# The q of one batch moves from VectorE to TensorE, later q transfers are halved, and an order is chosen anew

## The chip, the core and the metric

The kernel runs on one core of a Trainium2 chip. The metric is device time in microseconds (us), as the median of repeated executions. A profile is one execution taken by the hardware profiler; its span goes from the first to the last instruction. The engines are TensorE (PE, with PEld for its weight loads), VectorE (DVE), ScalarE (ACT), GpSimd (POOL) and SyncE (SP), which here issues nearly all DMAs.

## What is computed

An attention block without softmax feeds a two-layer network with a softplus between.

```python
batch, n_heads, seq, head_dim = (8, 8, 576, 64)
kv = np.einsum('bhsd,bhse->bhde', k, v)
out = np.einsum('bhsd,bhde->bhse', q, kv)
rms = np.sqrt(np.mean(out * out, axis=-1, keepdims=True) + 1e-06)
attn = out / rms * g_norm
x = attn.transpose(0, 2, 1, 3).reshape(4608, 512)
h = x @ w_in                                           # 512 x 2048
g = np.maximum(h, 0.0) + np.log1p(np.exp(-np.abs(h)))
result = g @ w_out                                     # 2048 x 512
```

The inputs q, k, v and g_norm are float32, the two weights float64.

## The kernel before

**Tiles.** The 4608 rows of x are 36 tiles of 128 rows; three tiles make a block of 384 (`NT`), and there are 12 blocks. A batch has 576 rows, four tiles and a half: batch 2 is tiles 9 to 12 and half of tile 13, batch 3 the other half of tile 13 and tiles 14 to 17. `parts(t)` says which batches a tile holds. `d_ff` is cut into 16 chunks of 128.

**Steps.** The network is walked in three phases over the blocks; `ENDS` says which chunks each phase does for each block. The first four blocks do chunks 0 to 3 in phase 0. One `step` is one block with one chunk: `mm1` (twelve matmuls, L660), softplus and a split into three parts on ACT and DVE, and `mm2` (nine matmuls, L667). Both products are made of three matmuls in a reduced form of float32, so x, the weights and g are each split into three terms. Partial results go to DRAM between phases. Steps 0 to 3 belong to block 0, 4 to 7 to block 1, 12 to 15 to block 3.

**Weights.** `weight(j, ...)` fetches one chunk of w_in (even j) or w_out (odd j), here named Wj, into one of two `raw` buffers (L283), turns float64 into float32 by several operations on DVE and ACT (L294 to L324), and `divide` splits it (L356 to L378; the first eight use two TensorE matmuls, L374 and L375).

**Attention.** `kv_of(b)` loads k and v of a batch into the ring `m` (L491, and tails L489) and multiplies them on TensorE (L502). `rows(t)` makes a tile of x: it needs q with the head dimension on the partitions (`qT`), multiplies it with kv (`out_rows`, L521, 32 matmuls into one of two `o` banks), squares on ACT (L590), reduces on DVE (L525), takes the root on POOL (L528, L529) and normalizes on DVE (L533). For tiles under `BY_PE` = 12 TensorE turns x (`turn_x`, L539); ACT copies it (L599) and SP stores it for later phases (L600). Tiles of the first two blocks (`AT_ONCE` = 6) are split from the turned tile directly; the others are loaded again (L638) and split (L445, L448, L452).

**How q is turned.** In batches 0 and 1 a tile's q is loaded by itself, in two transfers of rows of 64 floats (`load`, L567), turned by four TensorE transposes (`turn_q`, L577) into bank `tp`, or `o` from tile 6 on, and copied to `qT` by ACT (L584). From batch 2 on `load_q(b)` loads a whole batch into the one buffer `qa`, in four transfers of rows of 32 floats (L423), so that DVE can turn it with blocks of 32 x 32 (L552). Those loads follow each other, and none starts before `mm1` of a step set by `behind`.

**What sets the order.** The kernel is scheduled by hand: each piece of work is a `Task` with an engine, an estimated duration, a position `pos`, the buffers it takes and gives, and the tasks it comes after. `Plan.order` goes through the tasks as a list scheduler: an engine takes a task that could start within 150 ns (`SOON`) of the earliest possible, and of these the one with the lowest position. The result is a fixed order of instructions on each engine. SP may not run further than 2.5 us ahead of an estimated end of the DMAs (`dma_free`), and each DMA has an estimated length (`size`). Where TensorE would have nothing to do ahead of step 6, the plan puts in a filler matmul (`warm`, L778) whose result nobody reads.

**Positions.** They are counted in steps; negative ones are before step 0. They come from `P0`: eight for the conversion of the first eight weights (`CONVERT`), eight for their fetches (`FETCH`), eleven offsets for the attention and the loads (`EARLY`) and thirteen for the later weights (`LATER`). For instance `x_pos(t)` is `t * EARLY[0] + EARLY[1]` in block 0, and the first step of the tile's block less `EARLY[2]` (block 1) or `EARLY[3]` (later) plus the tile's index in its block; `kv_of` stands `EARLY[4]` ahead of the batch's first tile (`EARLY[5]` for batch 0) and loads `EARLY[6]` ahead of that; q is loaded `EARLY[7]` ahead of the tile, in `load_q` ahead of the batch's second tile. A load with `behind` = n waits for `mm1` of step n; a negative n is no wait.

Of the kernel before, what the change touches and what calls it, by code (L numbers as in the profile page):

```python
# [40 lines left out]
class Plan:  # L41
# [15 lines left out]
    def slot(self, ring):  # L57
        return Slot(ring)

    def add(self, engine, ns, run, after=(), pos=0.0, take=(), give=(), size=0, behind=None, follows=None):  # L60
        t = Task(engine, ns, run, [a for a in after if a is not None], pos, list(take), list(give), size)
        for s in t.give:
            s.readers += 1
        self.tasks.append(t)
        t.follows = follows
        t.behind = behind
        return t
# [79 lines left out]
def kernel(  # L147
# [25 lines left out]
    B, H, S, D = q.shape  # L173
# [3 lines left out]
    NP = H // 2  # L177
# [9 lines left out]
    PLACES = 8  # L187
    LAST = PHASES[-1]

    P0 = [-93.0, 0.8, -33.3, -5.7, -14.1, 1.5, -43.9, 2.2, -65.0, -42.8, -62.7, -19.7, -30.7, -6.2,  # L190
          -2.2, -4.7, 2.5, -26.5, 18.0, 10.5, 5.5, 8.5, -2.0, 2.5, 3.5, 25.5, -16.5, 10.0, 6.5, 41.0,
          52.0, 65.5, 54.5, 72.0, 91.5, 94.5, 115.5, 106.0, 111.5, 8.5]
    CONVERT, FETCH, EARLY, LATER = P0[:8], P0[8:16], P0[16:27], P0[27:]
    BY_PE = 12
    AT_ONCE = 2 * TB
# [27 lines left out]
    slot, add = plan.slot, plan.add  # L223

    def new(s, shape, dtype=F32):
        if s.ring == "o":
            s.tile = o_banks[:, :, s.place]
            return s.tile
        pool = ps if s.ring in PS else sb
        s.tile = pool.tile(shape, dtype, tag=f"{s.ring}_{s.place}", name=f"{s.ring}_{s.place}")  # L230
        return s.tile

    def pairs(x, p):

        return x[:, 2 * p:2 * p + 2].rearrange("r h d -> r (h d)")


    def halves(src, e):

        return src[e * NP:(e + 1) * NP].rearrange("p s d -> s p d")  # L240
# [155 lines left out]
    def parts(t):  # L396

        b, s0 = divmod(t * P, S)
        if s0 + P <= S:
            return [(b, 0, P, s0)]  # L400
        return [(b, 0, S - s0, s0), (b + 1, S - s0, P - S + s0, 0)]
# [8 lines left out]
    BL = 32  # L410
    q_slots, q_loads = {}, {}

    def load_q(b):


        q_slots[b], q_loads[b] = slot("qa"), []
        pos = x_pos(first_tile[b] + 1) - EARLY[7]

        def run(e, c):
            if not (e or c):  # L420
                new(q_slots[b], [P, NP * S])
            r0 = BL * (2 * e + c)
            nc.sync.dma_start(  # L423
                out=q_slots[b].tile[r0:r0 + BL].rearrange("j (i d) -> j i d", d=BL),
                in_=q[b, e * NP:(e + 1) * NP, :, BL * c:BL * (c + 1)].rearrange("p (i j) d -> j (p i) d", j=BL))

        for e in range(2):
            for c in range(2):
                q_loads[b].append(add("SP", 450, lambda e=e, c=c: run(e, c), (), pos + 0.2 * (2 * e + c),
                                      [q_slots[b]] if not (e or c) else [], [], 2190, behind=int(pos) - 3,  # L430
                                      follows=q_loads[b][-1] if e or c else None))

    def split(ph, t, x, ready, pos):
        n, i = divmod(t, TB)
# [33 lines left out]
    def x_pos(t):  # L468

        n = t // TB  # L470
        return t * EARLY[0] + EARLY[1] if n == 0 else first_step[0, n] - (EARLY[2] if n == 1 else EARLY[3]) + t % TB
# [36 lines left out]
    def rows(t):  # L508
        pos = x_pos(t)
# [31 lines left out]
        def part_of_qT(n, r0):  # L541
            if qT.tile is None:
                new(qT, [P, NP, P])
            return qT.tile[:, :, r0:r0 + n]

        turned = []
        for b, r0, n, s0 in parts(t):
            if b >= 2:
                if b not in q_slots:
                    load_q(b)  # L550
                turned.append(add(
                    "DVE", 690 if n == P else 420, lambda b=b, r0=r0, n=n, s0=s0: nc.vector.transpose(  # L552
                        out=part_of_qT(n, r0),
                        in_=q_slots[b].tile.rearrange("k (p s) -> k p s", p=NP)[:, :, s0:s0 + n]),
                    q_loads[b], pos - 1, [qT] if not r0 else [], [q_slots[b]], follows=turned[-1] if turned else None))
                continue

            if 0 not in q_slots:
                q_slots[0] = slot("qa")
            at_qa = n == P and b == 0  # L560
            q_s = q_slots[0] if at_qa else slot("m")

            def load(b=b, n=n, s0=s0, q_s=q_s, at_qa=at_qa):
                if q_s.tile is None:
                    new(q_s, [P, NP * S] if at_qa else [P, H, D])
                for e in range(2):
                    nc.sync.dma_start(out=natural(q_s, at_qa)[:n, e::2], in_=halves(q[b, :, s0:s0 + n], e))  # L567

            def natural(q_s, at_qa):
                if not at_qa:  # L570
                    return q_s.tile
                return q_s.tile[:, t * d_model:(t + 1) * d_model].rearrange("s (h d) -> s h d", d=D)

            def turn_q(n=n, q_s=q_s, at_qa=at_qa, tp=slot("tp" if t < AT_ONCE else "o")):
                y = new(tp, [P, NP, P])
                for p in range(NP):
                    nc.tensor.transpose(y[:, p, :n], pairs(natural(q_s, at_qa)[:n], p), ident[:n, :n])  # L577

            tp = turn_q.__defaults__[-1]
            ld = add("SP", 900, load, (), pos - EARLY[7], [q_s] if not at_qa or t == 0 else [], [], 1220 * n // P,  # L580
                     behind=int(pos) - 3, follows=first_load[0] if t and at_qa else None)
            first_load.append(ld)
            a = add("PE", 440, turn_q, [ld], pos - 1, [tp], [q_s])
            turned.append(add("ACT", 590, lambda n=n, r0=r0, tp=tp: nc.scalar.copy(part_of_qT(n, r0), tp.tile[:, :, :n]),  # L584
                              [a], pos - 1, [qT] if not r0 else [], [tp], follows=turned[-1] if turned else None))
        need = [u for pt in parts(t) for u in kv_ready[pt[0]]]
        a = o_task = add("PE", 640, out_rows, turned + need, pos, [o], [qT])
        for pt in parts(t):
            o_tasks.setdefault(pt[0], []).append(a)
        a = add("ACT", 600, lambda: nc.scalar.activation(new(x, [P, H, D]).rearrange("s (a k) d -> s a (k d)", k=2), o.tile, func=AF.Square,  # L590
                                                              scale=D ** -0.5), [a], pos, [x])
        a = add("DVE", 690, reduce, [a], pos, [r])
        a = add("POOL", 2300, root, [a], pos)
        a = add("DVE", 700, norm, [a, o_task], pos, [], [o, r])
        if t < BY_PE:
            a = add("PE", 440, turn_x, [a], pos + 0.5, [xp], [x])
            if t < AT_ONCE:
                split(0, t, xp, a, pos + 0.5)
            a = add("ACT", 600, lambda: nc.scalar.copy(new(xg, [P, KD, P]), xp.tile), [a], pos + 1, [xg], [xp])  # L599
            x_there[t] = [add("SP", 450, lambda: nc.sync.dma_start(  # L600
                out=x_of(t), in_=xg.tile), [a], pos + 1, [], [xg], 1000)]
# [4 lines left out]
        n, i = divmod(t, TB)  # L606
        g = TB if n < n_blocks - 1 else 1
        i0, i = i - i % g, i % g
# [21 lines left out]
    def x_of(t):  # L630

        n, i = divmod(t, TB)
        return xd[n][:, i * P:(i + 1) * P].rearrange("(a p) t -> p a t", p=P)
# [120 lines left out]
    for c in range(KF):  # L754
        for j in (2 * c, 2 * c + 1):
            pos = CONVERT[j] if c < 4 else LATER[c - 4] + LATER[12] * (j % 2)
            weight(j, pos, FETCH[j] if c < 4 else pos)
    for b in range(B):
        kv_of(b)
        for t in range(n_tiles):  # L760
            if parts(t)[-1][0] == b:
                rows(t)
# [51 lines left out]
```

## Time and profile before

| | us |
|---|---|
| median of 11 runs | 908.09 |
| lowest and highest of them | 907.17, 912.96 |
| the profiled execution | 912.96 |
| its span | 911.2 |
| `mm1` matmuls, L660, 2304 of them, busy | 436.3 |
| `mm2` matmuls, L667, 1728 of them, busy | 433.5 |
| filler, L778, 53 of them, busy | 20.5 |
| start of the first `mm1` | 42.66 |
| DVE transposes of q, L552, 24 whole, 6 halves, mean ns | 690, 427 |
| ACT copies of turned q, L584, from `tp`, from `o`, mean ns | 586, 594 |
| q of a batch, L423, 24 transfers of 288 KB, median us to landing | 7.3 |
| q of a tile, L567, into `m`: 8 of 128 KB and 4 of 64 KB, median us to landing | 4.3, 7.5 |

Busy times of TensorE contain overlaps at both ends of a group, and a matmul's duration is longer than its distance from the next. The row of a group names the line, the engine, what is written and read, and how many; in the chain of waits a piece is one after which the next could begin. The profiled execution is the longest of the eleven.

### The profile page before, as it was taken

Reading aid. Unit: us, or ns where it says so; the run is one execution under the profiler, and the core shown is the slowest. Engines: PE = TensorE matmul, PEld = TensorE weight load, DVE = VectorE, ACT = ScalarE, POOL = GpSimd, SP = SyncE. Lnnn points to the kernel's source line nnn. Section 1 sums busy time; section 2 is a strip of 40 time slices with the busy share of each in tenths; the row PEclk is TensorE's granted clock in tenths of the full one; section 3 lists DMA queues with packets and bytes.
Section 4 is the critical chain, followed back from the end, with each engine's and each line's share of the span. In section 5 each row is a group of like instructions: output and inputs, shape, how many; then the busy total and the mean of one; then the engine's idle time right before and its main releaser. Section 6 shows DMA issues by size and latency. Waiting matters only on the chain.

```text
span 911.2 us, 15563 instructions
## 1 busy us (share of the span) xinstructions
PE 895.5 (98%) x5983; PEld 790.7 (87%) x5983; DVE 624.0 (68%) x1054; ACT 408.3 (45%) x788; POOL 84.3 (9%) x79
## 2 busy tenths in 40 slices
PE   7899999999999999999999999999999999999998
PEld 5678888888888888999899998989999998999996
DVE  6786988676577877888668787886534555555553
ACT  5675654534444556654435544554323333333331
POOL 0433422223113200000000000000000000000000
PEclk8999999999999999999999999999999999999999
DMA  9999989479681635355343444741330433333323
GB/s 242 258 204 264 252 182 239 96 177 190 177 175 37 168 101 185 104 172 175 104 127 128 151 143 157 230 148 39 105 103 2 139 105 104 105 104 104 104 73 102
DMA packets 211451, 131.58 MB, mean 144 GB/s; under 512 B 102320, under 2 KB 185264, under 8 KB 211376
## 3 DMA queue, kind: packets, MB, share of 16 engines
q1 hardware_dynamic: 211216, 130.58, 52.7%
q8 instruction: 47, 0.77, 0.4%
q14 instruction: 28, 0.23, 0.1%
q10 hardware_dynamic: 160, 0.00, 0.0%
HBM read 91.75 MB, written 38.80 MB: 143 GB/s over the span
## 4 chain that ended last, share of the span: by engine, by line
PE 94%; DMA 4%; DVE 1%; ACT 0%; SPq 0%; issue 0%; DVEq 0%
PE h L660 45%; PE s L667 44%; DMA m<-in_v_dram 3%; PE o_banks L521 2%; PE tp L502 2%; DMA raw<-in_moe_w_in_dram 1%; DMA g_col<-in_g_norm_dram 1%; PE h L778 0%; PE o_banks L539 0%; DMA m<-in_k_dram 0%; PE tp L539 0%; SPq L491 0%; PE s L502 0%; ACT m L599 0%; PE tp L577 0%
## 5 line engine op out<-in xcount | busy, mean ns | idle before, releaser
L660 PE MATMUL h<-xv,w 128*128 128x384 f32 x2304 | 436.3, 338 | 0.2 <-ACT w L378 0.2
L667 PE MATMUL s<-w,gv 128*128 128x512 f32 x1728 | 433.5, 395 | 0.0
L660 PEld LDWEIGHTS h<-xv,w 128*128 128x128 f32 x2304 | 407.2, 188 | 16.4 <-ACT w L378 0.4
L667 PEld LDWEIGHTS s<-w,gv 128*128 128x128 f32 x1728 | 319.7, 188 | 60.4 <-DVE gv L675 0.2
L682 ACT ACTIVATE g<-h 128x384 f32<-128x384 f32 x192 | 94.3, 491 | 403.8 <-PE h L660 402.0
L671 DVE TENSOR_TENSOR gv<-g,gv 128x384 fp32r<-128x384 f32 x192 | 106.5, 554 | 181.1 <-ACT gv L684 180.0
L684 ACT ACTIVATE gv<-g 128x384 fp32r<-128x384 f32 x192 | 100.8, 525 | 24.7 <-PE s L667 18.5
L675 DVE SCALAR_TENSOR_TENSOR gv<-gv 128x384 fp32r<-128x384 f32 x192 | 106.8, 556 | 5.8
L448 DVE SCALAR_TENSOR_TENSOR xv<-m,g_col,xv 128x512 fp32r<-128x512 f32 x102 | 76.0, 745 | 2.3 <-ACT xv L445 2.3
L452 DVE SCALAR_TENSOR_TENSOR xv<-xv 128x512 fp32r<-128x512 f32 x108 | 74.3, 688 | 2.5
L445 ACT ACTIVATE xv<-m,g_down 128x512 fp32r<-128x512 f32 x102 | 70.1, 711 | 2.4 <-DMA m<-x 2.3
L529 POOL TENSOR_TENSOR r<-r,half 128x8 f32<-128x8 f32 x36 | 66.1, 1835 | 3.0
L533 DVE TENSOR_TENSOR x<-o_banks,r 128x512 f32<-128x512 f32 x36 | 24.8, 689 | 20.7 <-POOL r L529 8.4
L709 DVE SCALAR_TENSOR_TENSOR m<-s,scale,m 128x512 f32<-128x512 f32 x24 | 17.9, 747 | 29.7 <-PE s L667 29.7
L528 POOL TENSOR_SCALAR r<-r 128x8 f32<-128x8 f32 x36 | 17.3, 480 | 220.7 <-DVE r L525 220.3
L709 DVE SCALAR_TENSOR_TENSOR m<-s,m 128x512 f32<-128x512 f32 x36 | 23.7, 685 | 7.8 <-PE s L667 7.8
L521 PEld LDWEIGHTS o_banks<-kv,m 64*64 64x64 f32 x1152 | 20.2, 135 | 9.7 <-issue 5.5
L311 ACT ACTIVATE sq<-sq,big 128x512 bf16<-128x512 bf16 x32 | 22.9, 715 | 10.7 <-DVE m L307 10.7
L525 DVE TENSOR_REDUCE r<-x 128x8 f32<-128x512 f32 x36 | 24.2, 678 | 4.7 <-ACT x L590 4.7
L359 DVE TENSOR_TENSOR m<-m,w 128x512 f32<-128x512 f32 x30 | 20.6, 686 | 9.2 <-ACT w L356 8.8
L590 ACT ACTIVATE x<-o_banks 128x512 f32<-128x512 f32 x36 | 21.1, 593 | 12.5 <-PE o_banks L521 7.2
L521 PE MATMUL o_banks<-kv,m 64*64 64x64 f32 x1152 | 24.9, 226 | 0.8 <-ACT m L584 0.7
(71 smaller groups left out, 430.7 us busy)
## 6 DMA issues: line engine op xcount, KB each, us to landing
m<-x SPq DMA_DIRECT2D x102, 256.0 KB, 4.7
part<-m SPq DMA_DIRECT2D x72, 256.0 KB, 2.6
m<-part SPq DMA_DIRECT2D x72, 256.0 KB, 3.9
raw<-in_moe_w_in_dram SPq DMA_DIRECT2D x16, 512.0 KB, 5.3
m<-in_k_dram SPq DMA_DIRECT2D x32, 256.0 KB, 4.9
m<-in_v_dram SPq DMA_DIRECT2D x32, 256.0 KB, 4.8
raw<-in_moe_w_out_dram SPq DMA_DIRECT2D x16, 512.0 KB, 5.6
qa<-in_q_dram SPq DMA_DIRECT2D x24, 288.0 KB, 7.3
```

Of the source, the lines that this page charges most:

```text
L445: nc.scalar.activation(cols(0, F32R), x.tile, func=AF.Identity, scale=g_down)
L448: nc.vector.scalar_tensor_tensor(out=cols(1, F32R), in0=x.tile, scalar=g_col, in1=cols(0), op0=ALU.mult, op1=ALU.subtract)
L452: nc.vector.scalar_tensor_tensor(out=cols(2, F32R), in0=cols(1), scalar=-RADIX, in1=cols(0), op0=ALU.mult, op1=ALU.add)
L521: nc.tensor.matmul(y[r0:r0 + P // 2, a, c0:c0 + D], lhsT=qT.tile[e * D:(e + 1) * D, p, r0:r0 + P // 2], rhs=kvs[b % 2][e * D:(e + 1) * D, ...
L529: nc.gpsimd.tensor_tensor(out=r.tile, in0=r.tile, in1=half, op=ALU.pow)
L660: nc.tensor.matmul(hp, lhsT=w_in.tile[:, i, kd * P:(kd + 1) * P], rhs=xv.tile[:, i, kd], start=(m == 0), stop=(m == 3 * KD - 1))
L667: nc.tensor.matmul(mine[i].tile, lhsT=gv.tile[:, m, i * P:(i + 1) * P], rhs=w_out.tile[:, m], start=(c == cs[0] and m == 0), stop=(c == cs ...
L671: nc.vector.tensor_tensor(out=gv.tile[:, 1], in0=g.tile, in1=gv.tile.bitcast(F32)[:, 0], op=ALU.subtract)
L675: nc.vector.scalar_tensor_tensor(out=gv.tile[:, 2], in0=f32[:, 1], scalar=-RADIX, in1=f32[:, 0], op0=ALU.mult, op1=ALU.add)
L682: a = add("ACT", 490, lambda: nc.scalar.activation(new(g, [P, NT]), h.tile, func=AF.Softplus, scale=1.0 + E), [a], s, [g], [h])
L684: a = add("ACT", 530, lambda: nc.scalar.activation(new(gv, [P, 3, NT], F32R)[:, 0], g.tile, func=AF.Copy, scale=DOWN), [a], s, [gv])
L709: a = add("DVE", 700, lambda: nc.vector.scalar_tensor_tensor(out=new(ot, [P, d_model]), in0=bank.tile, scalar=(scale if ph == LAST else 1. ...
```

## The change

Three edits. `load_q` makes eight transfers a batch instead of four: each of the four groups of 32 partitions (`a`) is filled in two transfers of two head pairs (`p`), and the plan is told half the length for each. Its batches begin with 3 instead of 2, so the q of batch 2 is loaded and turned in the way of batches 0 and 1: five parts, each with two transfers, four TensorE transposes and an ACT copy, in the ring `m` and, for the turned tile, an `o` bank. And 23 of the 40 numbers in `P0` are different.

```diff
-    P0 = [-93.0, 0.8, -33.3, -5.7, -14.1, 1.5, -43.9, 2.2, -65.0, -42.8, -62.7, -19.7, -30.7, -6.2,
-          -2.2, -4.7, 2.5, -26.5, 18.0, 10.5, 5.5, 8.5, -2.0, 2.5, 3.5, 25.5, -16.5, 10.0, 6.5, 41.0,
-          52.0, 65.5, 54.5, 72.0, 91.5, 94.5, 115.5, 106.0, 111.5, 8.5]
+    P0 = [-88.5, 0.8, -46.3, -8.2, -11.1, 2.0, -42.9, 2.7, -64.0, -43.8, -63.7, -16.7, -31.2, -9.7, 0.3,
+          -4.7, 5.0, -33.5, 16.5, 10.5, 5.5, 8.5, -2.0, 2.5, 3.5, 26.0, -22.0, 10.0, 4.5, 41.0, 50.0,
+          65.5, 54.5, 72.0, 91.5, 94.5, 114.5, 106.0, 109.5, 8.5]
...
-        def run(e, c):
-            if not (e or c):
+        def run(a, p):
+            if not (a or p):
                 new(q_slots[b], [P, NP * S])
-            r0 = BL * (2 * e + c)
+            e, c = divmod(a, 2)
             nc.sync.dma_start(
-                out=q_slots[b].tile[r0:r0 + BL].rearrange("j (i d) -> j i d", d=BL),
-                in_=q[b, e * NP:(e + 1) * NP, :, BL * c:BL * (c + 1)].rearrange("p (i j) d -> j (p i) d", j=BL))
-
-        for e in range(2):
-            for c in range(2):
-                q_loads[b].append(add("SP", 450, lambda e=e, c=c: run(e, c), (), pos + 0.2 * (2 * e + c),
-                                      [q_slots[b]] if not (e or c) else [], [], 2190, behind=int(pos) - 3,
-                                      follows=q_loads[b][-1] if e or c else None))
+                out=q_slots[b].tile[BL * a:BL * (a + 1), p * S:(p + 2) * S].rearrange("j (i d) -> j i d", d=BL),
+                in_=q[b, e * NP + p:e * NP + p + 2, :, BL * c:BL * (c + 1)].rearrange("p (i j) d -> j (p i) d", j=BL))
+
+        for a in range(4):
+            for p in range(0, NP, 2):
+                q_loads[b].append(add("SP", 500, lambda a=a, p=p: run(a, p), (), pos + 0.1 * (2 * a + p // 2),
+                                      [q_slots[b]] if not (a or p) else [], [], 1095, behind=int(pos) - 3,
+                                      follows=q_loads[b][-1] if a or p else None))
...
-            if b >= 2:
+            if b >= 3:
```

## The prediction

> **What bounds the kernel now.** I read the page's busy rows and its 40 slices first, then busy time by stretch, then the chain of waits, then the instructions of SP and of TensorE in order of time.
>
> ```profile
> PE 895.5 (98%) x5983; PEld 790.7 (87%) x5983; DVE 624.0 (68%) x1054; ACT 408.3 (45%) x788; POOL 84.3 (9%) x79
> PE   7899999999999999999999999999999999999998
> DMA  9999989479681635355343444741330433333323
> ```
>
> TensorE sets the time: 895.5 of 911.2 us. The DMA engines are full in the first slices and loose later. Where TensorE still has room is seen by stretch (columns: length; busy us of PE, PEld, DVE, ACT, POOL; granted clock; DMA share; GB/s):
>
> ```profile
> 0.00:42.00 42.00, 33.31 (x373) 22.75 (x373) 29.25 (x53) 23.07 (x44) 10.34 (x15) 0.88 0.95 247
> 42.00:76.40 34.40, 32.05 (x372) 26.49 (x373) 26.78 (x46) 23.56 (x48) 9.89 (x8) 0.95 0.97 229
> 76.40:130.00 53.60, 53.49 (x604) 45.98 (x604) 45.09 (x77) 32.39 (x62) 17.96 (x16) 1.00 0.90 233
> 130.00:260.00 130.00, 130.00 (x1216) 112.02 (x1214) 93.65 (x158) 55.35 (x107) 32.18 (x28) 1.00 0.79 174
> ```
>
> From 76.4 us on TensorE has no gap. Part of its earlier busy time is filler: `warm` (L778). The same stretches for that line alone (busy us of PE, PEld; clock; DMA):
>
> ```profile
> 0.00:42.00 42.00, 18.44 (x47) 9.70 (x47) 0.88 0.95 247
> 42.00:76.40 34.40, 2.03 (x7) 1.05 (x6) 0.95 0.97 229
> ```
>
> So the room is 8.7 idle + 18.4 filler = 27.1 us before the first `mm1` (42.7 us), and 2.35 + 2.03 = 4.4 us from there to 76.4. Nothing that only moves work after 76.4 us can shorten the run, and each TensorE instruction added there lengthens it. The chain of waits (start, length, what) shows what ended last in the second stretch:
>
> ```profile
> 59.61 0.54 SPq L491
> 60.15 0.05 issue
> 60.20 0.02 SPq L491
> 60.21 0.03 issue
> 60.24 7.38 DMA m<-in_v_dram
> 67.62 0.14 issue
> 67.75 0.69 PE tp L502 x16
> 68.44 3.37 PE h L660 x12
> 71.81 1.05 PE tp L502 x16
> ```
>
> A load of v, issued at 60.24, lands at 67.62; TensorE's kv matmuls (L502) wait for it, and `mm1` of step 3 stands behind them. SP's issues tell why v was late:
>
> ```profile
> 49.86 0.45 SPq L491 DMA_DIRECT2D m<-in_v_dram  x1
> 50.36 6.82 SPq L423 DMA_DIRECT2D qa<-in_q_dram  x2
> 57.28 1.20 SPq L600 DMA_DIRECT2D x<-m  x1
> 58.57 0.45 SPq L491 DMA_DIRECT2D m<-in_k_dram  x1
> ...
> 60.71 6.40 SPq L423 DMA_DIRECT2D qa<-in_q_dram  x2
> ```
>
> The four transfers of batch 2's q hold SP for 6.82 + 6.40 = 13.2 us; k and v of the same batch stand behind the first two.
>
> **What the change does, part by part.** Batch 2 is rows 1152 to 1727: tiles 9 to 12 whole and half of tile 13, five parts.
>
> *TensorE, added.* Five `turn_q`, 20 transposes. Four of them are 0.44 us on the chain behind other transposes and 0.62 behind other matmuls; 5 x 0.44 to 5 x 0.62 is 2.2 to 3.1 us. I take 2.6, between the two because both neighbours occur. They fall around and after 60 us; if they land in a gap that is left, they cost nothing, so the range goes from 0 to 3.1. The Trainium skill, "TensorE: Matmul & The Clock Gate", Part 4 (PE-mode transpose), gives about 275 ns for a 128x128 transpose inside a kernel; 20 x 0.275 would be an estimated 5.5 us and with it the change would come out level. This trace has one each 0.11 to 0.155 us, and the row is nearer than the page.
>
> *ACT, added; DVE, removed.* The copies at L584 take 0.585 to 0.599 us (0.37 for a half): 4 x 0.59 + 0.37 = 2.7 us on ACT, busy 6.4 of 10 us at 80 to 90. DVE loses 4 x 0.69 + 0.43 = 3.2 us of L552 between 74 and 87 us. TensorE has its next work in hand there, so I cost both at nothing; without this cover the one takes 2.7 and the other gives 3.2.
>
> *DMA, the main term.* From 50.4 to 67.2 us the windows give 193, 197 and 189 GB/s, about 3.2 MB, where 269 GB/s follow from 68 to 80. The q of a batch is 1.18 MB; the other 2.0 MB at 269 GB/s need 7.5 us, so q took some 9.3 us in rows of 128 bytes. By tiles, in rows of 256 bytes, only tiles 9 to 11 are loaded early: 0.79 MB at the 241 GB/s of 30 to 50 us, 3.3 us. Tiles 12 and 13 get places 3 and 4 and may start only after `mm1` of steps 2 and 3. So about 6 us of DMA leave the stretch 50 to 67 us, and v, now 1.7 us late, is there in time. What then goes: 1.74 idle at 66.0, about 0.2 more of idle there, 2.03 of filler, and the slow clock behind the gap (granted 0.55 in 69 to 72 us: `mm1` 3.37 for 2.28 us, L502 1.05 for 0.62, together 1.5). Sum 5.5 us at most. I take all of it, since the cover needed (1.7 us of DMA) is a third of what leaves.
>
> *Eight transfers a batch.* SP issues 10 + 40 where it issued 24: 26 more by 0.43 to 0.51 us, 11 to 13 us spread to about 260 us, while TensorE is without a gap. Cost nothing; if the cover were gone, some 0.5 us for each that stands before a load that is waited for. Batch 3's q is different: the `qa` buffer, read last by the turns at 31 us, is now free for it, its place is 5.0 and it waits only for `mm1` of step 2 (51.3 us), where before it was issued from 87.75 us. The Trainium skill ("DMA: Bandwidth & Descriptors", Bandwidth) asks for transfers of 1 MiB and calls small ones descriptor-dominated, which speaks against halving 288 KB, with no price for two that overlap. In SP's rows two of the 288 KB transfers were issued within 2.91 us at 92.45, while one takes 7.3 us (median) to land: they overlap, and I let the split cost no more than the same packets before.
>
> *Buffers.* q of tiles 9 to 13 now takes places of the 13-deep ring `m` and a third use of the two `o` banks. Behind a waiting `out_rows` or `turn_q` stand `mm1` and `mm2`, in TensorE's one queue. Tiles 6 to 8 already use the banks so; their waits are 0.2 us (0.21 at 62.72). Five times that is 1.0 us above, nothing below; I take nothing, as tile 9's rows are needed only at step 12.
>
> *Positions.* By rank, most of the start stays: W0, W2, W1, k and v of batch 0, W4 with q of tiles 0 to 2, W3, batch 1. Three things shift: the W4 conversion goes from before the rows of tile 3 (-14.1 against -14.0) to behind tile 4 (-11.1 against -11.5); W5's fetch is earlier (-6.2 to -9.7); W6's fetch, issued at 49.39, goes behind batch 2's k and v and the q of tiles 9 and 10 (-2.2 to 0.3). The trace has no run of this order. Bounds: in the instructions of DVE and TensorE tile 1 is normalized at 31.2 and turned only at 34.4, behind kv of batch 1 that waits 1.69 us for its v, and tile 2 is normalized at 38.3 and turned at 39.6: 3.1 + 1.2 = 4.3 us to gain at most; on the other side a W4 pushed by two tiles' reduce and norm (2 x 1.4 us on DVE) is 2.8 us of loss. I take nothing: `mm1` 0 needs neither W4 nor W5.
>
> **Sum.** Profiled execution 912.96 us, of which the span is 911.2 and 1.8 lies around it: 912.96 - 5.5 + 2.6 = 910.1. The median of the 11 runs is 908.09, 4.9 below the profiled one; the difference of -2.9 carried to it gives **905.2**.
>
> **Rivals.** *The relief is given back* (chance 0.20). SP takes whatever has its buffer, and batch 3's q needs no place in `m`: it may fill the hole that batch 2's q leaves, with 9.3 us of packets beside the 3.3 of the tiles. For it: `qa` is free and the wait is only on step 2. Against it: its place, 5.0, is behind all of batch 3's k and v. Then half of the 5.5 is won and 2.6 paid: 908.0.
>
> *A weight comes late; slower* (0.28). W6 now is fetched at 49.39 and its last conversion on ACT (L378) ends at 64.7, 3.7 us before `mm1` of step 3 starts. Issued behind k and v of batch 2, that is at 60.2, it would be 10.8 us later and `mm1` 3 would wait 10.8 - 3.7 = 7.1 us; other TensorE work fills about half. With the 2.6 of turns: 908.1 + 3.5 + 2.6 = 914 at worst, 911.5 if half of the 5.5 is still won. It decides from a fetch of W6 later than about 53 us. Against it: its raw buffer and SP are free while k and v wait for places in `m`.
>
> *The start gains as well* (0.17): the turn of tile 1 no longer stands behind kv of batch 1, 3.1 us more: 902.1. For it, their places are now 5 apart and earlier by 4.5 and 2; against it, their rank did not change.
>
> *My forecast* has 0.35. About 0.2%, 1.8 us, is what a measurement of this kernel can tell from no change. Faster takes the forecast, but for a small part, and the third rival: 0.50; same 0.20; slower 0.30. The likeliest case alone runs from 902.6 (5.5 won, nothing paid) to 907.5; the whole range, with the bounds of the positions, **900 to 912**.
>
> **What would show it.** Right: 20 more matmuls at L577; the L502 of batch 2 without a wait for v; no filler and a granted clock near 1.00 from 60 to 76 us; TensorE without a gap by about 73 us. Wrong: batch 3's q issued before 70 us with SP held for several us at L423; W6's fetch after 53 us and `mm1` of step 3 waiting for ACT; new TensorE waits at `o_banks`; a first `mm1` more than 3 us away from 42.7, which would make the positions the main term; or gaps after 80 us, of which I cost none.

## The result: slower by half a per cent, and the profile after

The changed kernel takes 912.71 us (median of 11 runs, 911.79 to 915.62); the kernel before, over 41 runs, 908.36. The ratio is 1.0048, 95% interval [1.0036, 1.0060]: 4.4 us slower, and above the predicted 900 to 912. The profiled executions say the opposite at first sight: a span of 910.6 after, 911.2 before. The page of the kernel after, busy rows and slices:

```profile
PE 898.0 (99%) x6005; PEld 790.9 (87%) x6005; DVE 621.9 (68%) x1049; ACT 411.5 (45%) x793; POOL 85.6 (9%) x79
PE   7999999999999999999999999999999999999998
DMA  9999767959681636355343445650320433433323
```

TensorE is busy for 2.5 us more, DVE for 2.1 less. By stretch of the kernel after (length; busy us of PE, PEld, DVE, ACT, POOL; clock; DMA share; GB/s):

```profile
0.00:42.00 42.00, 34.59 (x389) 24.45 (x390) 31.85 (x58) 25.16 (x48) 10.95 (x15) 0.92 0.99 262
42.00:76.40 34.40, 33.92 (x420) 27.72 (x422) 29.66 (x50) 25.66 (x52) 12.30 (x10) 1.00 0.99 250
76.40:130.00 53.60, 52.81 (x606) 43.87 (x597) 42.78 (x72) 33.22 (x64) 18.40 (x16) 1.00 0.80 214
130.00:260.00 130.00, 130.00 (x1193) 111.42 (x1184) 88.31 (x149) 53.19 (x102) 29.97 (x26) 1.00 0.78 170
```

and for the fillers, L778, alone (busy us of PE, PEld; clock; DMA):

```profile
42.00:76.40 34.40, 2.45 (x8) 1.42 (x8) 1.00 0.99 250
```

From 42 to 76.4 us the idle time fell as forecast, to 0.48 us, and the granted clock stays at 1.00. But there are eight fillers now, not none, and from 76.4 to 130 there is 0.79 us of idle where there was 0.11. The instructions of TensorE after (start, us, what, idle before and its releaser) show the place:

```profile
68.64 0.60 PE L539 MATMUL o_banks<-ident_r,x 128*128 128x128 f32 x4
68.99 1.83 PE L778 MATMUL h<-ident_r 128*128 128x512 f32 x6
71.03 0.66 PE L577 MATMUL o_banks<-ident_r,m 128*128 128x128 f32 x4 [0.21 <-ACT m L599]
...
77.96 0.66 PE L577 MATMUL o_banks<-ident_r,m 128*128 128x128 f32 x4 [0.31 <-ACT x L590]
```

The turned x of a tile occupies an `o` bank until ACT has copied it (L599); `turn_q` of the next tile stands in TensorE's queue for that bank. Six fillers and 0.21 us of idle precede it at 71.0. The wait at 77.96 ends with another reader of these banks, ACT's squares (L590). SP's issues after, of the q loads among others:

```profile
48.34 1.34 SPq L423 DMA_DIRECT2D qa<-in_q_dram  x1
49.77 2.45 SPq L491 DMA_DIRECT2D m<-in_k_dram  x1
52.28 0.86 SPq L423 DMA_DIRECT2D qa<-in_q_dram  x1
...
56.84 0.67 SPq L423 DMA_DIRECT2D qa<-in_q_dram  x1
57.62 0.97 SPq L283 DMA_DIRECT2D raw<-in_moe_w_in_dram  x1
...
65.32 0.47 SPq L423 DMA_DIRECT2D qa<-in_q_dram  x1
```

Half of batch 3's q, four of its eight transfers, is in the hole that batch 2's left, as one rival said, but one transfer at a time: a q load holds SP for 1.34 us at most in these rows, where two of them held it for 6.82 and 6.40 us before.

### The profile page after: what moved, and what is told of

It is laid out like the page before. It is cut to its first block, busy times and chain, and to the rows that moved or that the text cites. A ratio compares the mean times of both kernels' runs of the same rounds, so it can differ in the third digit from the quotient of the medians.

```text
span 910.6 us, 15638 instructions
## 1 busy us (share of the span) xinstructions
PE 898.0 (99%) x6005; PEld 790.9 (87%) x6005; DVE 621.9 (68%) x1049; ACT 411.5 (45%) x793; POOL 85.6 (9%) x79
## 4 chain that ended last, share of the span: by engine, by line
PE 96%; DMA 2%; ACT 1%; issue 0%; DVE 0%; SPq 0%; DVEq 0%
PE h L660 45%; PE s L667 44%; PE o_banks L521 2%; PE tp L502 2%; DMA m<-in_v_dram 2%; PE h L778 1%; PE s L502 1%; PE o_banks L577 0%; PE o_banks L539 0%; PE tp L539 0%; PE h L374 0%; PE tp L577 0%; ACT m L584 0%; ACT x L590 0%; ACT m L599 0%
## 5 line engine op out<-in xcount | busy, mean ns | idle before, releaser
L521 PEld LDWEIGHTS o_banks<-kv,m 64*64 64x64 f32 x1152 | 20.1, 134 | 8.9 <-issue 5.5
L521 PE MATMUL o_banks<-kv,m 64*64 64x64 f32 x1152 | 25.0, 224 | 0.6 <-ACT m L584 0.5
L590 ACT ACTIVATE x<-o_banks 128x512 f32<-128x512 f32 x36 | 21.3, 593 | 8.6 <-DVE x L533 4.0
```

The lines of the kernel that those rows point to most:

```text
L521: nc.tensor.matmul(y[r0:r0 + P // 2, a, c0:c0 + D], lhsT=qT.tile[e * D:(e + 1) * D, p, r0:r0 + P // 2], rhs=kvs[b % 2][e * D:(e + 1) * D, ...
```

## The experiments

Seven runs part the three edits; four measure the turn, its bank and batch 3's q; the last tried for a version better than both. Each was timed in five rounds against the kernel before on the same chip.

| run | positions | transfers | batch 2's q turned by | median us | ratio to before, 95% |
|---|---|---|---|---|---|
| before again | old | 4 | DVE | 908.50 | 0.9996 [0.9983, 1.0009] |
| eight only | old | 8 | DVE | 908.76 | 0.9995 [0.9983, 1.0007] |
| positions only | new | 4 | DVE | 912.27 | 1.0041 [1.0026, 1.0056] |
| positions and eight | new | 8 | DVE | 909.57 | 1.0004 [0.9993, 1.0015] |
| turns only | old | 4 | TensorE | 912.57 | 1.0049 [1.0032, 1.0066] |
| turns and eight | old | 8 | TensorE | 912.41 | 1.0038 [1.0024, 1.0051] |
| turns and positions | new | 4 | TensorE | 912.44 | 1.0042 [1.0026, 1.0058] |
| all three (the change) | new | 8 | TensorE | 912.71 | 1.0048 [1.0036, 1.0060] |

Every row with the turns on TensorE is at 912.4 to 912.7, with either set of positions and either count of transfers. Of the others only one is slower than before.

**The kernel before, again.** No edit.

> The kernel before, unchanged, profiled again. Theory A (the profiled execution of before was one of its slowest, 4.9 us over the median, and its gap at 66.0 to 67.7 us with the slow clock behind it is not in a usual execution): ratio 1.000 within 0.001, a span of 906 to 907 us, first mm1 near 40 us instead of 42.7, no wait for v over 0.5 us from 60 to 70 us, granted clock near 1.00 from 68 to 76. Theory B (the gap belongs to every execution of before, and the change is slower for other reasons): the wait of about 1.7 us and a clock below 0.9 there again.

Its span is 906.8 us and its profiled execution took 908.57, at the median. The start comes earlier here, so the same stretch of the clock holds a slightly later part of the work. By stretch, and below that the fillers alone:

```profile
42.00:76.40 34.40, 31.69 (x426) 26.08 (x423) 27.62 (x47) 22.68 (x46) 12.79 (x12) 1.00 1.00 235
76.40:130.00 53.60, 53.49 (x589) 45.66 (x588) 45.20 (x77) 33.25 (x64) 16.46 (x15) 1.00 0.96 234
```

```profile
42.00:76.40 34.40, 1.96 (x6) 1.05 (x6) 1.00 1.00 235
```

In the order of TensorE's instructions, this profile and then two rows of the first one:

```profile
39.10 2.35 PE L660 MATMUL h<-xv,w 128*128 128x384 f32 x12
...
62.03 0.69 PE L502 MATMUL tp<-m,m 128*64 128x64 f32 x16 [1.28 <-DMA m<-in_v_dram]
...
64.94 0.69 PE L502 MATMUL tp<-m,m 128*64 128x64 f32 x16 [0.88 <-DMA m<-in_v_dram]
65.55 2.36 PE L660 MATMUL h<-xv,w 128*128 128x384 f32 x12
```

```profile
67.75 0.69 PE L502 MATMUL tp<-m,m 128*64 128x64 f32 x16 [1.74 <-DMA m<-in_v_dram]
68.37 3.44 PE L660 MATMUL h<-xv,w 128*128 128x384 f32 x12
```

Half of theory A holds. The first `mm1` starts at 39.1, not at 42.7, and no slow clock follows: `mm1` of step 3 takes 2.36 us, not 3.44. The first profile is 4.4 us longer, though the instructions and their order are the same. But waits for v, 1.28 and 0.88 us, are here too, against what theory A expected; they belong to the kernel.

**Positions only.** The diff of `P0` as shown with the change, nothing else.

> The kernel before with the new positions alone. Theory A with the loss in the turns: within 0.1% of before (907 to 909.5). Theory W (a weight comes late by the new positions): most of the 4.4 us loss, 911 to 913.

Slower by 3.7 us, as the rival of a weight that comes late says, in this combination. SP's issues, then TensorE's instructions:

```profile
55.49 0.42 SPq L491 DMA_DIRECT2D m<-in_v_dram  x1
55.96 0.46 SPq L283 DMA_DIRECT2D raw<-in_moe_w_in_dram  x1
```

```profile
66.39 3.78 PE L778 MATMUL h<-ident_r 128*128 128x512 f32 x12
70.59 0.69 PE L502 MATMUL tp<-m,m 128*64 128x64 f32 x16 [0.41 <-DMA m<-in_v_dram]
71.20 0.50 PE L374 MATMUL h<-w,ident_r 128*128 128x512 f32 x1
...
74.08 2.37 PE L660 MATMUL h<-xv,w 128*128 128x384 f32 x12
```

W6 is fetched at 55.96 (46.73 in the repeated profile of before), is split by TensorE at 71.2, and `mm1` of step 3 starts at 74.1 instead of 65.6, behind twelve fillers. That W6 is the cause is read from these rows; no run moves its fetch alone. In the changed kernel W6 is fetched at 47.17 and that step starts at 63.2: there this rival did not happen.

**Turns only.**

```diff
-            if b >= 2:
+            if b >= 3:
```

> The kernel before with only batch 2 turned by TensorE, old positions, four transfers. Theory A with the loss in the turns: 2.5 to 5 us above before (910.5 to 913). Theory W: at most 1 us above before.

The loss is all there, without the new positions. **Four transfers in the changed kernel** (`load_q` as before):

> The changed kernel with four transfers a batch instead of eight. If the split of the transfers costs nothing, the same as the changed kernel, 912 to 913.5; if the eight transfers hurt, nearer to 909.

The same as the changed kernel: the split into eight is not what costs. **Eight transfers only:**

> The kernel before with only the eight transfers a batch. If TensorE is without a gap wherever they run, and they cost nothing: 907.5 to 909. If the finer transfers let k and v through earlier: 1 to 2 us faster, 906 to 907. If they hold SP: over 910.

As before: the interval goes from 0.17% less to 0.07% more. **The changed kernel with batch 2 turned by DVE again** (`b >= 2`):

> The changed kernel with batch 2's q again loaded whole and turned by DVE. Theory A with the loss in the turns: as before or a little faster, 906 to 909. Theory W (positions): 911 to 913.

Undoing the one line takes away 0.44 of the 0.48%, though 909.57 lies a little above the 906 to 909 that were expected. With eight transfers the new positions are harmless; with four (positions only) they are not. **The changed kernel with the old positions:**

> The changed kernel with the old positions. Theory A with the loss in the turns: 910.5 to 914, the changed kernel's loss or more, since the positions were not fitted to it. Theory W: 908 to 909.5.

The loss stays. **The turns done twice**, in the same order of instructions:

```diff
-            def turn_q(n=n, q_s=q_s, at_qa=at_qa, tp=slot("tp" if t < AT_ONCE else "o")):
+            def turn_q(b=b, n=n, q_s=q_s, at_qa=at_qa, tp=slot("tp" if t < AT_ONCE else "o")):
                 y = new(tp, [P, NP, P])
-                for p in range(NP):
+                for p in [*range(NP)] * (2 if b == 2 else 1):
                     nc.tensor.transpose(y[:, p, :n], pairs(natural(q_s, at_qa)[:n], p), ident[:n, :n])
```

> The changed kernel with the 20 TensorE transposes of batch 2 done twice in the same order. If a transposed tile costs TensorE its 0.44 us where it has no gap: 20 more x 0.11 = 2.2 us over the changed kernel, 914.5 to 915.2, so that 2.2 of the 4.4 us loss are the matmuls themselves. If they fall in gaps: 913 or less.

915.24 us, ratio 1.0063 [1.0046, 1.0080]. The median is 2.5 above the changed kernel's and so is the time from the first `mm1` to the end of the span (913.3 - 40.16 = 873.1 against 910.6 - 39.96 = 870.6), though the two intervals overlap. Not all of the 2.5 in the profiles is the transposes: from start to start the 20 take 1.9 us more at L577 (5.99 against 4.08, without idle time). A wait of 0.90 us for v at 56.2, ahead of the first doubled turn, is in this profile and not in that of the changed kernel. The added transposes are paid for all the same.

**Turns by themselves**, added to the kernel before where TensorE has nothing but large matmuls:

```diff
+    def alone(s):
+        y = new(s, [P, NP, P])
+        for p in range(NP):
+            nc.tensor.transpose(y[:, p], ident, ident)
+
+    for s in range(100, 140, 2):
+        bank = slot("tp")
+        add("PE", 440, lambda bank=bank: alone(bank), [mm1s[s]], s + 0.2, [bank], [bank])
```

> The kernel before with 20 added groups of four 128x128 TensorE transposes of the identity, one in every second step from step 100 on, where TensorE has no gap and no other small matmul; their results are not used. Theory S (a turn standing alone costs its 0.44 us and 0.17 to 0.2 more, because the next large matmul after a float32 group starts slower, 2.28 instead of 2.10 us for mm1): 20 x 0.61 to 0.64 = 12.2 to 12.8 us over before, and the profile shows 2.28 behind each group. Theory M (only the matmuls count): 20 x 0.44 = 8.8 us.

917.88 against 908.34: 9.5 us, ratio 1.0100 [1.0082, 1.0118], for 20 groups 0.48 each (0.37 to 0.54 by the interval), and theory S falls. The chain of waits at one of them:

```profile
515.21 2.10 PE h L660 x12
517.31 0.70 PE s L667 x3
518.01 0.44 PE tp L776 x4
518.45 1.38 PE s L667 x6
519.82 2.10 PE h L660 x12
```

A whole turn of four costs 0.44 us in all: `mm2`, cut in two, takes 0.70 + 1.38, its usual 2.08. The 2.28 us of other `mm1` come from what stands before them; the last section shows it.

**The turned q in an h bank:**

```diff
-            def turn_q(n=n, q_s=q_s, at_qa=at_qa, tp=slot("tp" if t < AT_ONCE else "o")):
+            def turn_q(n=n, q_s=q_s, at_qa=at_qa, tp=slot("tp" if t < AT_ONCE else "h" if b == 2 else "o")):
```

> The changed kernel with the turned q of batch 2 in an h bank instead of an o bank, so that no turn waits for an o bank. Theory O (the o banks' third use costs fillers, idle time and broken-up mm2 groups): 1 to 2 us below the changed kernel, 910.7 to 911.7. If the o banks cost nothing: 912.3 to 913, and the loss is the turns and their switches alone.

910.52, ratio 1.0022 [1.0010, 1.0034]; the interval lies below that of the changed kernel. Theory O holds, a little beyond its range: half of the loss goes with the bank. By stretch in this run, and the fillers alone:

```profile
42.00:76.40 34.40, 32.85 (x428) 27.61 (x428) 29.23 (x49) 25.95 (x53) 13.38 (x12) 1.00 1.03 245
76.40:130.00 53.60, 53.52 (x599) 45.21 (x599) 45.14 (x76) 33.08 (x64) 15.46 (x15) 1.00 0.89 230
```

```profile
42.00:76.40 34.40, 1.50 (x4) 0.75 (x4) 1.00 1.03 245
```

Between 42 and 76.4 us the fillers fall by 0.95 us, but idle time rises from 0.48 to 1.55. The bank decides more than these waits: the whole planned order from 60 to 100 us is another, so 2.2 us is the price of the bank together with the order that it forces. No run separates the two.

**Batch 3's q late:**

```diff
-                                      [q_slots[b]] if not (a or p) else [], [], 1095, behind=int(pos) - 3,
+                                      [q_slots[b]] if not (a or p) else [], [], 1095, behind=int(pos) - 3 + (5 if b == 3 else 0),
```

> The changed kernel with batch 3's q held until mm1 of step 7, near the time it was loaded before the change. Theory G (batch 3's q fills the hole that batch 2's leaves, and its small rows hold back k, v and the tiles' q): 1 to 2.5 us below the changed kernel, 910.2 to 911.7, less filler from 58 to 72 us. If the early load costs TensorE nothing: 912.3 to 913.

It is issued from 93.3 us on, the fillers between 42 and 76.4 go down to three, and the time is 913.44, ratio 1.0054 [1.0039, 1.0069]: no gain. A new wait shows in TensorE's instructions, for x that is split late:

```profile
77.09 0.66 PE L577 MATMUL o_banks<-ident_r,m 128*128 128x128 f32 x4 [0.74 <-ACT m L599]
...
143.46 3.06 PE L660 MATMUL h<-xv,w 128*128 128x384 f32 x16 [1.44 <-DVE xv L452]
```

So the run does not settle it: the fillers fall from 2.45 to 1.28 us, and these two waits are 2.18 us. Holding the load back wins nothing in sum; what the early load costs by itself stays open.

**A try for more.** If the third use of the `o` banks costs, the kernel before might gain by moving the turn of x out of them:

```diff
-        tp, qT, o, x, r, xp, xg = (slot(n) for n in ("tp", "m", "o", "x", "r", "tp" if t < AT_ONCE else "o", "m"))
+        tp, qT, o, x, r, xp, xg = (slot(n) for n in ("tp", "m", "o", "x", "r", "tp" if t < AT_ONCE else "h", "m"))
```

> The kernel before, with x of tiles 6 to 11 turned by TensorE into an h bank instead of an o bank; batch 2's q stays with DVE. Theory O (the third use of the o banks is what costs): the planned order has 4 fillers after the first mm1 instead of 6 and 44 instead of 47 changes from a 64-row matmul to another kind, worth 2 x 0.4 + 3 x 0.18 = 1.3 us: 906.5 to 908, faster than both kernels. If the o banks are a bottleneck only with the third user of the change: 908 to 909.5, as before.

910.08, ratio 1.0014 [0.9999, 1.0029]: not faster, and above both expectations. In its instructions TensorE waits 1.98 us for v at 66.4, so fewer fillers in the planned order did not turn into time. No run is faster than the kernel before.

## Why the prediction was wrong

**What bounds the kernel: right.** TensorE without a gap from some 76 us on, and each instruction added there is paid in full (20 turns added between 517 and 686 us cost 0.48 each).

**The turns, 2.6 us: right in size.** Five turns at 0.44 by themselves are 2.2 us, and the trace of the changed kernel has 2.4 more at L577. The 0.62 "behind other matmuls" rests on one row, a half turn behind a filler at 37.97; behind `mm2` a turn takes 0.44.

**The step that failed: "I take all of it", 5.5 us to win.** Of its three parts two were not there to be had. (1) 2.03 us of it were fillers. These are instructions in a fixed order, put in where the plan's own estimate has a hole; a DMA that lands earlier on the chip can't remove them. Only another planned order does, and the one with the change has eight behind the first `mm1` instead of six: 2.45 us. (2) 1.5 us were the slow clock, which the second profile of the same kernel doesn't show. (3) What is in the kernel is the wait for v, and it went: idle between 42 and 76.4 us fell from 2.71 in the repeated profile to 0.48, 2.2 us, of which 0.7 came back between 76.4 and 130. So 5.5 shrank to 1.6 of idle time, less 0.7 for the two more fillers, by the account below: 0.9 us.

**Carrying the difference to the median.** The profiled execution stood 4.9 us above the median, and the text said so without asking what those 4.9 us were. The repeated profile answers: 3.6 in the first `mm1` (42.66 against 39.10) and 0.8 behind it (868.5 against 867.7 us from there to the end of the span) make the 4.4 us between the two spans. A room measured in the slowest of eleven executions was offered to the median one.

**Buffers, "I take nothing": wrong.** The bound of 1.0 came from the wait of 0.21 at 62.72. That wait ends with ACT's copy of a turned q (L584), which `out_rows` needs as its input in any case, so it sets no price on a bank. With five more turns in them, the `o` banks and the order that they force cost 2.2 us, shown by the run with the h bank. New waits at `o_banks` were named as a sign of being wrong, and they came, but they are only 0.8 of it (0.21, 0.31 and 0.30 at L577); the fillers and the order that the plan makes of it are the rest.

**Positions, "I take nothing": right in this kernel,** since old and new ones give the same time with the turns (912.41 and 912.71), and with eight transfers and DVE's turn (908.76 and 909.57, intervals that overlap). The late weight was a real danger: with four transfers the new positions cost 3.7 us. There W6 was fetched at 55.96, beyond the 53 us that the rival gave.

**Batch 3's q.** That it would fill the hole was right for half of it. Whether this gives relief back is open: held back, nothing is won, but new waits come with it. **Eight transfers at nothing: right.** **DVE and ACT at nothing:** no run shows a gain from DVE's 3.2 us of saved turns, and what ACT's copies cost alone was not tried.

**The account.** From the first `mm1` to the end of the span the changed kernel takes 870.6 us, the kernel before 867.7 in its repeated profile: 2.9 more. Added up from the traces, from the start of each matmul to the start of the next and less idle time, it closes. The sum goes to the start of the same kv tail (an L502 at 256.70, 261.06 and 258.27 in the order of the columns); the columns are in us, with the number of matmuls where it differs.

| from the first `mm1` | before, repeated | changed | turned q in an h bank |
|---|---|---|---|
| turns of q, L577 | 1.72 (16) | 4.08 (36) | 3.84 (36) |
| `mm1` and `mm2`, 822 matmuls | 170.48 | 172.14 | 171.08 |
| other matmuls of attention and weights | 40.85 | 41.21 | 41.22 |
| fillers | 1.73 (6) | 2.40 (8) | 1.26 (4) |
| idle | 2.82 | 1.26 | 1.63 |
| sum | 217.60 | 221.09 | 219.02 |
| from there to the end of the span | 650.08 | 649.51 | 649.50 |

The term that the prediction did not have is 1.7 us in `mm1` and `mm2` themselves. The same matmuls are cut more often: 1.1 of it lies next to matmuls of L502 and L521, in 79 places instead of 68 at about 0.1 us each, and most of the rest next to transposes. The 0.6 us less in the last row lies behind the last matmul. What is left to 4.4 is the first `mm1`, 0.9 later than in the repeated profile, less than it varies between two executions of one kernel, and some 0.6 by which the two profiled executions differ from their medians.

## What to carry to other kernels

Before a gap in a profile is priced, profile the same kernel a second time if the profiled execution lies away from the median; only what both show belongs to the kernel. Work that a static plan puts in as filler is no slack of the chip: ask whether the order changes, not whether the wait goes. When an operation is moved to the engine that sets the time, count the buffer that it shares there as well as its instructions; here the instructions cost 2.4 us, and the buffer with the order that it forced 2.2.

## What was not expected of the hardware

Four 128x128 float32 transposes between large matmuls cost 0.44 us in all (0.70 + 1.38 us of `mm2` around them). The longer time of 2.28 instead of 2.10 us for an `mm1` stands in these traces behind the matmuls of L502 (128*64) and L521 (64*64), and a turn behind one of them takes 0.58 to 0.60 instead of 0.44. The chain of waits of the changed kernel, then of the kernel before in its repeated profile:

```profile
102.08 0.62 PE o_banks L521 x32
102.70 2.28 PE h L660 x12
104.98 2.08 PE s L667 x9
107.06 2.08 PE h L660 x12
```

```profile
68.52 0.62 PE o_banks L521 x32
69.15 0.58 PE tp L539 x4
69.73 0.70 PE s L667 x3
70.43 0.44 PE o_banks L539 x4
```

So the 0.18 us goes with the small matmuls, and not with transposes as such. These matmuls use a smaller part of the array and also stream only 64 columns; no run separates the two. The Trainium skill ("TensorEngine Tiling (Array Packing)", Key Properties) says that a change of tiling mode drains the engine; these rows are consistent with that, at 0.18 us, but no run shows a drain.

The same instructions in the same order started their first `mm1` at 42.66 us in one execution and at 39.10 in another. Between 30 and 39 us the DMA engines moved 182 GB/s in the first and 247 in the second. Two waits of the first, together 2.5 of the 3.6 us, are not in the second:

```profile
30.32 0.69 PE L502 MATMUL s<-m,m 128*64 128x64 f32 x16 [0.84 <-DMA m<-in_v_dram]
...
33.76 0.69 PE L502 MATMUL s<-m,m 128*64 128x64 f32 x16 [1.69 <-DMA m<-in_v_dram]
```
